# A state-space convolution and SwiGLU kernel on one core: a planned order that knows DMA lanes and dependent VectorE steps, merged opening loads, and the last product written over the kernel spectrum

## The chip, the cores and the metric

One Trainium2 chip, one core. The metric is the device time of one execution in microseconds (us), lower is better; several executions of each kernel are timed, and one further look is taken with the hardware profiler. Names used below: PE is TensorE (matmul), DVE is VectorE, ACT is ScalarE, POOL is GpSimd, SP is the engine that issues most DMA. The profile's *span* runs from the first to the last instruction and is some 1.8 us shorter than the device time of the same run.

An execution is called *fast* when it is within 1.5% of the fastest run of the same kernel, else *slow*; only fast runs are compared.

## The reference, cut to what matters

```python
# one batch, S = 2048 rows, D = 640, F = 1728, bf16
kv  = shift_conv4(k, shift_k) * v                 # 4-tap causal shift along S, then times v
y   = causal_conv(kv, ssm_k) + kv * ssm_D         # long convolution along S (written with rfft/irfft)
h   = q + layernorm(q) * y
out = h + (silu(layernorm(h) @ w_gate) * (layernorm(h) @ w_up)) @ w_down
```

## The kernel before

The sequence is cut into four blocks of 512 rows. The long convolution is done by block: each block of kv gets a trigonometric transform X(n) by matmul, each block of the kernel gets one G(p), combined into H(p), and the spectrum of output block n is A(n) = the sum of X(j)*H(n-j). Such a complex product of two 128x2560 halves is six or eight VectorE operations (`pair`). An inverse transform, two layer norms and an FFN follow for every block.

All instructions are first recorded in a plan with an engine, an estimated duration, dependencies and a priority. A greedy planner then simulates them and emits one fixed order for each engine; on the chip every engine works through its own list in that order. So the planner's model decides what stands behind what.

```python
    def order(self):                                   # the planner, cut
        free, dma, out = {}, 0.0, []
        while len(out) < n:
            # ... of all ready operations take the one that can start first, then by priority
            end = s + o["dur"]
            if o["kb"]:                                # a DMA: one common queue
                dma = max(dma, end + 1.3) + o["kb"] / RATE      # RATE = 270
                done = dma + 0.7
            for u in users[i]:                         # same engine: no delay
                lag = 0.0 if ops[u]["eng"] == e and not o["kb"] else 0.12
```

```python
    H = [slot[0], slot[4], slot[2], slot[3]]           # spectra of the kernel
    X = [slot[5], slot[6], slot[5], slot[6]]           # spectra of kv: X(2) reuses X(0)'s slot
    A = [slot[6], slot[7], slot[1], slot[7]]           # sums of products: A(3) reuses A(1)'s
    # ... pair(), the eight-operation form; T is one 128x2560 scratch tile
            vop(TM, T, U, U2, "T", xk + "c", gk + "c", pr)      # T  = U*U2
            vop(TA, Ac, Ac, T, ak + "c", "T", ak + "c", pr)     # Ac = Ac + T, reads what was just written
            vop(TM, T, V, V2, "T", xk + "s", gk + "s", pr)
            vop(TS, Ac, Ac, T, ak + "c", "T", ak + "c", pr)
            # ... the same twice more for As
```

Because X(2) needs X(0)'s slot, the products X(0)*H(2) and X(0)*H(3) have to be out of the way before X(2); the loop places them, and the products of X(1), right after the inverse transforms of blocks 1 and 2. Nothing but X(3)*H(0) is then left for block 3.

The opening loads k and v in one load a row tile, WG (the basis of G) in two halves, and the flip (a matrix that mirrors rows), WX (the basis of X) and x (the rows of q) loads with early priorities, most of them on ACT's queue, which also has to copy w4 (the broadcast shift weights) out of PSUM before VectorE can start.

## Time and profile before

| | before |
|---|---|
| median of the first three runs (range) | 335.8 us (332.1 to 337.7) |
| span of the profiled run | 328.4 us |
| first product of spectra on VectorE starts | 48.2 us |
| last spectral operation ends | 262.1 us |
| from there to the end | 66.3 us |

Busy time by stretch of the kernel before: opening, product stretch, end. Columns are the stretch and its length, then for each engine the busy us and the instruction count, then TensorE's granted clock (1.00 is full speed), the busy share of the DMA engines and GB/s.

```profile
core 0: us, PE busy (x) PEld busy (x) DVE busy (x) ACT busy (x) POOL busy (x), PEclk, DMA share, GB/s
0.00:48.20 48.20, 25.08 (x129) 14.79 (x130) 18.09 (x24) 21.41 (x40) 11.21 (x27) 0.93 0.95 256
48.20:262.10 213.90, 186.65 (x1065) 104.35 (x1077) 200.54 (x246) 121.87 (x233) 60.77 (x88) 0.97 0.47 133
262.10:328.40 66.30, 60.58 (x348) 32.98 (x350) 20.17 (x40) 23.15 (x46) 5.59 (x16) 1.00 0.30 78
```

In the middle line VectorE is busy 200.5 of 213.9 us and TensorE 186.7: VectorE bounds the stretch. In the last line it is TensorE alone. The total is the sum of the three lengths, so anything that moves the end of the second line moves the end of the kernel.

ACT's timeline in the opening of the kernel before. Columns: start, length, engine (ACTq is its DMA issue), source line, operation, and in brackets the idle time of ACT's compute before it with what ended it.

```profile
16.22 0.39 ACTq L252 DMA_DIRECT2D x<-in_A_q_dram  x1
16.64 1.28 ACT L278 ACT_TABLE_LOAD   x1 [16.64 <-DMA v<-in_A_v_dram]
17.94 1.29 ACT L278 CAST w<-psA 128x640 bf16<-128x640 f32 x2
...
26.02 0.34 ACTq L252 DMA_DIRECT2D WI<-const_wi  x1
26.40 1.29 ACT L294 CAST s0c<-psF 128x640 bf16<-128x640 f32 x2 [5.68 <-DMA wd<-in_A_ssm_k_dram]
```

ACT stands behind its own loads: the w4 copies come after the issue of x at 16.2, and the next copies after the issue of WI, which does not get out until 26.0.

VectorE in the product stretch of the kernel before:

```profile
106.35 1.49 DVE L356 TENSOR_TENSOR s<-s,T 128x2560 bf16<-128x2560 bf16 x1
107.76 0.42 DVE L494 TENSOR_TENSOR tT<-sg,uc 128x512 bf16<-128x512 bf16 x1
108.10 1.48 DVE L356 TENSOR_TENSOR T<-s6s,s0s 128x2560 bf16<-128x2560 bf16 x1
109.61 1.49 DVE L356 TENSOR_TENSOR s<-s,T 128x2560 bf16<-128x2560 bf16 x1
```

A 128x2560 operation takes 1.40 us start to start when the next does not need its result (106.35 to 107.76 shows 1.41), and 1.52 us when the next one reads it (108.10 to 109.61 shows 1.51). I call the difference, 0.115 us, a bubble. The step can be counted in a timeline: it is where the next operation starts after the printed end of the one before, by less than 0.15 us. There are 81 of them in the product stretch.

VectorE at the last X transform, then TensorE at the start of the third FFN, both of the kernel before:

```profile
245.94 0.43 DVE L494 TENSOR_TENSOR tT<-sg,uc 128x512 bf16<-128x512 bf16 x1 [4.92 <-ACT uc L492]
248.70 1.49 DVE L356 TENSOR_TENSOR T<-s6c,s0c 128x2560 bf16<-128x2560 bf16 x1 [2.33 <-ACT s6c L352]
```

```profile
205.68 0.45 PE L335 MATMUL psA<-kv,flip 128*128 128x320 bf16 x2
215.84 0.58 PE L485 MATMUL psF<-hT,wg 128*128 128x512 bf16 x1 [9.71 <-DVE s L356]
```

VectorE idles 4.92 and 2.33 us because no product is left to do; earlier, TensorE idles 9.71 us because the third FFN's input, hT, waits in VectorE's list.

### The profile page before, as it was taken

The numbers are of one execution on the slowest core, as the hardware profiler recorded it, in microseconds if no ns is written. First come the engines' busy times: TensorE is split into PE (matmuls) and PEld (weight loads), VectorE is DVE, ScalarE is ACT, GpSimd is POOL, SyncE is SP. The second block draws the span as 40 slices with busy tenths as digits, with TensorE's granted clock in tenths as the row PEclk, the third lists the DMA queues.
The fourth block names the chain that finished last, engine by engine and source line by source line (L and its number), as shares of the span: only waits on it lengthen the run. The fifth ranks groups of instructions, "written<-read, shape, count | busy, mean of one in ns | idle before, by whom it ended". The sixth has DMA issues, their size and how long they took to land.

```text
span 328.4 us, 4290 instructions
## 1 busy us (share of the span) xinstructions
PE 272.3 (83%) x1540; PEld 152.1 (46%) x1556; DVE 238.8 (73%) x307; ACT 166.4 (51%) x318; POOL 77.6 (24%) x131
## 2 busy tenths in 40 slices
PE   1066789995899988999989799169997998999995
PEld 0034546773345444654445366024453564444563
DVE  0049359998999999999999999999836984121122
ACT  0043998876256548116768217268465472355400
POOL 5000333650000004800580004579300033000000
PEclk9997979999799999999999999769999999999999
DMA  7999930239673507229992701516732405365011
GB/s 220 353 196 310 351 73 1 103 60 299 222 212 98 142 4 177 63 79 289 276 283 56 221 21 40 147 35 160 232 84 53 113 23 130 90 161 141 0 42 40
DMA packets 72121, 45.94 MB, mean 140 GB/s; under 512 B 30821, under 2 KB 69542, under 8 KB 72100
## 3 DMA queue, kind: packets, MB, share of 16 engines
q1 hardware_dynamic: 70160, 41.22, 45.9%
q10 hardware_dynamic: 1812, 4.38, 4.3%
q8 instruction: 12, 0.20, 0.2%
q0 software_dynamic: 128, 0.07, 0.1%
q14 instruction: 9, 0.07, 0.1%
HBM read 37.80 MB, written 2.62 MB: 123 GB/s over the span
## 4 chain that ended last, share of the span: by engine, by line
DVE 44%; PE 24%; issue 5%; ACT 4%; POOL 3%; DMA 1%; POOLq 0%; ACTq 0%; DVEq 0%; SPq 0%
PE psF L485 18%; DVE T L356 8%; DVE s L356 8%; DVE k L321 4%; PE psF L503 4%; DVE tT L494 2%; DVE k L322 2%; DVE s1s L356 2%; DVE o L508 2%; DVE s1c L356 2%; ACT uc L492 1%; DVE kv L324 1%; PE psA L349 1%; DVE x L452 1%; DVE k L323 1%
## 5 line engine op out<-in xcount | busy, mean ns | idle before, releaser
L485 PE MATMUL psF<-hT,wg 128*128 128x512 bf16 x269 | 70.6, 386 | 20.9 <-DVE s L356 9.7
L491 ACT ACTIVATE sg<-psF 128x512 bf16<-128x512 f32 (+1 forms) x56 | 33.4, 597 | 80.8 <-PE psF L485 76.6
L503 PE MATMUL psF<-wd,tT 128*128 128x320 bf16 x448 | 66.4, 299 | 1.2 <-ACT uc L492 1.2
L485 PE MATMUL psF<-hT,wu 128*128 128x512 bf16 x255 | 65.8, 386 | 0.8 <-ACT sg L491 0.4
L404 POOL TENSOR_TENSOR sm<-sm 128x1 f32<-128x1 f32 x28 | 13.9, 497 | 169.4 <-ACT junk L397 169.4
L503 PEld LDWEIGHTS <-tT 128*128 128x128 bf16 x448 | 41.5, 97 | 25.4 <-issue 8.7
L485 PEld LDWEIGHTS <-wg 128*128 128x128 bf16 x280 | 27.3, 99 | 53.8 <-issue 25.7
L494 DVE TENSOR_TENSOR tT<-sg,uc 128x512 bf16<-128x512 bf16 (+1 forms) x56 | 23.4, 419 | 34.7 <-ACT uc L492 34.5
L485 PEld LDWEIGHTS <-wu 128*128 128x128 bf16 x260 | 25.9, 100 | 31.6 <-issue 3.7
L492 ACT CAST uc<-psF 128x512 bf16<-128x512 f32 (+1 forms) x56 | 32.5, 580 | 3.7 <-PE psF L485 3.6
L291 PE MATMUL psF<-wd,s 128*128 128x320 bf16 x192 | 31.4, 325 | 3.3 <-ACT s0c L294 2.8
L291 PEld LDWEIGHTS <-s 128*128 128x128 bf16 x256 | 26.4, 104 | 16.2 <-issue 4.4
L321 DVE TENSOR_TENSOR k<-k,w 128x2560 bf16<-128x2560 bf16 x14 | 20.7, 1484 | 14.7 <-ACT w L278 14.7
L356 DVE TENSOR_TENSOR s<-s,T 128x2560 bf16<-128x2560 bf16 x20 | 29.8, 1488 | 0.4
L407 POOL TENSOR_TENSOR sm<-sm,mhalf 128x1 f32<-128x1 f32 x32 | 26.8, 837 | 2.7
L397 ACT ACTIVATE junk<-x 128x640 bf16<-128x640 bf16 x28 | 20.6, 737 | 10.5 <-DMA x<-in_A_q_dram 6.5
L349 PE MATMUL psA<-kv,WX 128*128 128x320 bf16 x128 | 21.5, 316 | 3.9 <-DVE kv L339 2.7
L508 DVE TENSOR_TENSOR o<-psF,x 128x640 bf16<-128x640 f32 x16 | 13.1, 819 | 12.3 <-PE psF L503 12.3
L398 ACT ACTIVATE junk<-x 128x640 bf16<-128x640 bf16 x28 | 20.7, 738 | 0.5
L349 PEld LDWEIGHTS <-WX 128*128 128x128 bf16 x128 | 13.1, 103 | 12.5 <-issue 3.0
L406 POOL TENSOR_SCALAR sm<-sm 128x1 f32<-128x1 f32 x28 | 17.8, 635 | 2.6 <-POOL sm L405 0.2
L405 POOL TENSOR_TENSOR sm<-sm 128x1 f32<-128x1 f32 x28 | 13.0, 464 | 18.2 <-ACT junk L398 17.1
(107 smaller groups left out, 309.4 us busy)
## 6 DMA issues: line engine op xcount, KB each, us to landing
k<-in_A_k_dram SPq DMA_DIRECT2D x12, 640.0 KB, 4.2
wg<-in_B_w_gate_dram SPq DMA_DIRECT2D x24, 320.0 KB, 3.2
wu<-in_B_w_up_dram SPq DMA_DIRECT2D x24, 320.0 KB, 3.8
out_dram<-o SPq DMA_DIRECT2D x16, 160.0 KB, 1.8
wd<-in_B_w_down_dram SPq DMA_DIRECT2D x1, 2080.0 KB
v<-in_A_v_dram SPq DMA_DIRECT2D x12, 160.0 KB, 4.2
x<-in_A_q_dram SPq DMA_DIRECT2D x3, 640.0 KB
s<-const_wg ACTq DMA_DIRECT2D x2, 512.0 KB, 8.7
```

Of the source, the lines that this page charges most:

```text
L291: nc.tensor.matmul(ps(g)[:, h, 0:NH], WG[:, kt, ct * P:(ct + 1) * P], gT[p][:, kt, h * NH:(h + 1) * NH], start=(kt == 0), stop=(kt == 3))
L321: add("DVE", dve(4 * D), lambda: nc.vector.tensor_mul(kd[:], kd[:], w4[:]), r=["w4"] + ks, w=[kn], pr=pr)
L349: nc.tensor.matmul(ps(g)[:, h, 0:NH], WX[:, kt, ct * P:(ct + 1) * P], kv[:, base + kt, h * NH:(h + 1) * NH], start=(kt == 0), stop=(kt == 1))
L356: add("DVE", dve(4 * D), lambda: f(o[:], a[:], b[:]), r=[ak, bk], w=[ok], after=["WG0", "WG1"] if ok[:2] == "s7" else [], pr=pr)
L397: add("ACT", act(D) + 0.2, lambda: nc.scalar.activation(junk[:], src, ACT.Copy, scale=1.0 / D, accum_out=s[:, 0:1]), r=[xk], w=[k + "a"], ...
L398: add("ACT", act(D) + 0.2, lambda: nc.scalar.activation(junk[:], src, ACT.Square, scale=float(D ** -0.5), accum_out=s[:, 1:2]), r=[xk], w= ...
L407: e.tensor_tensor(s[:, 4:5], s[:, 3:4], mhalf[:], op=ALU.pow)
L485: nc.tensor.matmul(ps(gr)[:, which, :], w[:, kt, cc * P:(cc + 1) * P], hT[b][:, kt, :], start=(kt == 0), stop=(kt == 4))
L491: add("ACT", act(MB), lambda gr=gr, s=s, z=z: nc.scalar.activation(sg[s][:z, :], ps(gr)[:z, 0, :], ACT.Silu), r=[(gr, 0)], w=[f"sg{s}"], p ...
L492: add("ACT", act(MB), lambda gr=gr, s=s, z=z, merged=merged: nc.scalar.copy(uc[s][:z, :], ps(gr)[64:128, 0, :] if merged else ps(gr)[:, 1, ...
L494: add("DVE", dve(MB), lambda c=c, s=s, z=z: TM(tT[:z, c * MB:(c + 1) * MB], sg[s][:z, :], uc[s][:z, :]), r=[f"sg{s}", f"uc{s}"], w=[f"tT{c ...
L503: nc.tensor.matmul(ps(gr)[:, h, 0:NH], tT[:z, c * MB + m * P:c * MB + (m + 1) * P], wd[:z, c, h * NH:(h + 1) * NH], start=(c == 0), stop=( ...
```

## The change

Its intent: make the planner (a) hold a load back until one of eight *lanes* is free (a lane is taken by each load not issued by POOL, until it has landed) and let the queues share one bandwidth; (b) start a dependent VectorE operation 0.12 us late, as the traces show it, so that independent ones are put between; (c) merge the loads of the opening so that fewer issues block ACT; (d) write the last product X(0)*H(3) over H(3), so that X(2), X(3) and A(3) get free slots and all products of a block but the last one can be done before its own X transform.

```diff
-        free, dma, out = {}, 0.0, []
+        free, dma, out, lanes = {}, {}, [], [0.0] * 8
+                    if o["kb"] and e != "POOL":
+                        s = max(s, lanes[0])
-                dma = max(dma, end + 1.3) + o["kb"] / RATE
-                done = dma + 0.7
+                begin = max(dma.get(e, 0.0), end + 1.3)
+                share = 1 + sum(f > begin for q, f in dma.items() if q != e)
+                dma[e] = begin + o["kb"] * share / RATE
+                done = dma[e] + 0.7
+                if e != "POOL":
+                    lanes = lanes[1:] + [done]
-                lag = 0.0 if ops[u]["eng"] == e and not o["kb"] else 0.12
+                lag = 0.0 if ops[u]["eng"] == e and e != "DVE" and not o["kb"] else 0.12
-RATE = 270.0
+RATE = 330.0
+MOVE = "add"
-    T = tl("T", [P, 4, D])
+    T = tl("T", [P, 8, D])          # two halves, Ta and Tb
-    X = [slot[5], slot[6], slot[5], slot[6]]
-    A = [slot[6], slot[7], slot[1], slot[7]]
+    X = [slot[5], slot[6], slot[7], slot[5]]
+    A = [slot[6], slot[7], slot[1], slot[3]]
# ... opening: SP's transposes are planned with 2.7 us of issue instead of 4.5; WG in one 1 MB load, v of block 0 in one load, k rows 256 to 511 in one 1.28 MB load,
# ... ssm_D moved to POOL's queue, an early Silu so that the table load comes first, t0 for flip, WX, WI
# ... pair(): products and sums alternate between Ta and Tb; "over" writes A over H(3);
# ... a variant that lets DMA do the additions is in the code, but MOVE = "add" leaves it unused
-                add("PE", ..., mm, r=["wdl", "wdl2"] + ...)
+                add("PE", ..., mm, r=["wdl", "wdl2", (("F", "U", n, 13), 0)] + ...)   # down after the last up
     for n in range(1, NB):
         front(n, z)
-        if n == 1:
-            pair(0, 1, z + 20, True)
         load_x(n, z - 100)
-        if n == 2:
-            pair(0, 3, z + 5, True)
+        pair(0, n, z + 20, "over" if n == 3 else "first")
+        for j in range(1, n):
+            pair(j, n - j, z + 22 + j, MOVE)
         x_transform(n, z + 30)
-        pair(n, 0, z + 40, False)
+        pair(n, 0, z + 40, "add")
         inverse(n, z + 50)
-# ... the products that stood here after the inverse are gone
```

More of the change, by code (lines that the diff above doesn't have):

```diff
@@ L109, in order @@
             if best is None:
-                for i, o in enumerate(ops):
-                    if "start" not in o: print(i, o["eng"], o["pr"], o["acq"], left[i], o["fn"].__qualname__, o["fn"].__code__.co_firstlineno)
                 raise RuntimeError("stuck")
@@ L191 @@
     J_h = nc.inline_tensor(make_flip(), name="const_flip")
-    slot = [[tl(f"s{i}{h}", [P, 4, D]) for h in "cs"] for i in range(7)]
-    last = tl("s7", [P, 8, D])
-    slot.append([last[:, 0:4, :], last[:, 4:8, :]])
-    T = tl("T", [P, 4, D])
+    slot = [tl(f"s{i}", [P, 8, D]) for i in range(8)]
+    last, fourth = slot[7], slot[4]
+    slot = [[t[:, 0:4, :], t[:, 4:8, :]] for t in slot]
+    T = tl("T", [P, 8, D])
+    Tk = [["T0", "T1"], ["T2", "T3"]]
     tT = tl("tT", [P, 14 * MB])
@@ L202 @@
     w4 = tl("w4", [P, 4, D])
-    wrow = T[0:1, :, :].rearrange("p a b -> p (a b)")
+    wrow = T[0:1, 0:4, :].rearrange("p a b -> p (a b)")
     ones = tl("ones", [1, P])
@@ L236 @@
     G = [slot[0], slot[1], slot[2], slot[3]]
-    X = [slot[5], slot[6], slot[5], slot[6]]
-    A = [slot[6], slot[7], slot[1], slot[7]]
+    X = [slot[5], slot[6], slot[7], slot[5]]
+    A = [slot[6], slot[7], slot[1], slot[3]]
     Hk, Gk = ["s0", "s4", "s2", "s3"], ["s0", "s1", "s2", "s3"]
-    Xk, Ak = ["s5", "s6", "s5", "s6"], ["s6", "s7", "s1", "s7"]
+    Xk, Ak = ["s5", "s6", "s7", "s5"], ["s6", "s7", "s1", "s3"]
     def r3(a):
@@ L257 @@
     load("ACT", wrow, A_shift_k.partition_broadcast(1).rearrange("o a b -> o (a b)"), ["wrow"], -100, 5)
-    load("ACT", drow, A_ssm_D.partition_broadcast(1), ["drow"], -99, 5)
+    add("ACT", 1.5, lambda: nc.scalar.activation(sg[0][0:1, 0:P], ones[:], ACT.Silu), r=["ones"], w=["sg0"], pr=-50)
+    load("POOL", drow, A_ssm_D.partition_broadcast(1), ["drow"], -75, 5)
     def gload(p, pr):
-        add("SP", 4.5, lambda: nc.sync.dma_start_transpose(gT[p], A_ssm_k[:, p * MB:(p + 1) * MB]), w=[f"gT{p}"], pr=pr, kb=640)
-    def wgload(i):
-        load("ACT", WG[:, 2 * i:2 * i + 2, :], WG_h.ap()[:, 2 * i:2 * i + 2, :], [f"WG{i}"], -39.5 + i, 512)
+        add("SP", 2.7, lambda: nc.sync.dma_start_transpose(gT[p], A_ssm_k[:, p * MB:(p + 1) * MB]), w=[f"gT{p}"], pr=pr, kb=640)
     gload(0, -90)
-    wgload(0)
-    wgload(1)
     def wcast(t):
@@ L299, in front_loads, with front_tile @@
         pass
-    def front_tile(n, q, pr, queue):
+    def front_tile(n, q, pr):
         b = q % 2
         r0 = n * MB + q * P
-        kd, kn = k4[b], f"k4_{b}"
-        if n == 0 and q > 1:
-            kd, kn = slot[4][b], "s4" + "cs"[b]
-        if n == 0 and q == 0:
-            add("POOL", 0.8, lambda: nc.gpsimd.memset(kd[0:32, :, :], 0.0), w=[kn], pr=-8)
-            for t in range(3):
-                k = 3 - t
-                load("POOL", kd[t:t + 1, k:4, :], kk[0:t + 1, :].rearrange("(o a) d -> o a d", o=1), [kn + f"x{t}"], -7, 2, r=[kn])
-            load("POOL", kd[3:16, :, :], bass.AP(tensor=kk.tensor, offset=kk.offset, ap=[[D, 13], [1, 4 * D]]).rearrange("p (a b) -> p a b", a=4), [kn + "x3"], -7, 65, r=[kn])
-            load(queue, kd[16:128, :, :], bass.AP(tensor=kk.tensor, offset=kk.offset + 13 * D, ap=[[D, 112], [1, 4 * D]]).rearrange("p (a b) -> p a b", a=4), [kn + "x4"], pr - 40, 560)
-        else:
-            load(queue, kd[:], bass.AP(tensor=kk.tensor, offset=kk.offset + (r0 - 3) * D, ap=[[D, P], [1, 4 * D]]).rearrange("p (a b) -> p a b", a=4), [kn] + [kn + f"x{i}" for i in range(5)], pr - 40, 640)
-        vb, vn = vt[b], f"v{b}"
-        if n == 0 and q > 1:
-            vb, vn = ot[b], f"o{b}"
-        load(queue, vb[:], vv[r0:r0 + P, :], [vn], pr - 40, 160)
-        ks = [kn] + [kn + f"x{i}" for i in range(5)]
+        kd, kn, vb, vn = k4[b], f"k4_{b}", vt[b], f"v{b}"
+        if n == 0:
+            vb, vn = hT[0][:].rearrange("p a b -> p (a b)")[:, q * D:(q + 1) * D], "v0all"
+            if q > 1:
+                kd, kn = slot[4][b], "s4" + "cs"[b]
+        else:
+            load("SP", kd[:], run(r0 - 3, P), [kn], pr - 40, 640)
+            load("SP", vb[:], vv[r0:r0 + P, :], [vn], pr - 40, 160)
+        ks = [kn] + [f"edge{i}" for i in range(5) if n == 0 and q == 0]
         add("DVE", dve(4 * D), lambda: nc.vector.tensor_mul(kd[:], kd[:], w4[:]), r=["w4"] + ks, w=[kn], pr=pr)
@@ L324, in front_tile, with run, first_loads, front @@
         add("DVE", dve(D), lambda: nc.vector.tensor_mul(kv[:, q, :], kd[:, 0, :], vb[:]), r=ks + [vn], w=[f"kv{q}"], pr=pr)
-    def front(n, pr, queue="SP"):
+    def run(row, n):
+        return bass.AP(tensor=kk.tensor, offset=kk.offset + row * D, ap=[[D, n], [1, 4 * D]]).rearrange("p (a b) -> p a b", a=4)
+    def first_loads():
+        kd = k4[0]
+        load("ACT", kd[16:128, :, :], run(13, 112), ["edge4"], -98, 560)
+        load("SP", k4[1][:], run(P - 3, P), ["k4_1"], -88, 640)
+        load("ACT", hT[0][:].rearrange("p a b -> p (a b)").rearrange("p (a b) -> p a b", a=4), vv[0:MB, :].rearrange("(m p) d -> p m d", p=P), ["v0all"], -97, 640)
+        load("ACT", WG, WG_h.ap(), ["WG0", "WG1"], -96, 1024)
+        load("SP", fourth[:].rearrange("p (m a) b -> p m (a b)", m=2),
+             bass.AP(tensor=kk.tensor, offset=kk.offset + (2 * P - 3) * D, ap=[[D, P], [P * D, 2], [1, 4 * D]]), ["s4c", "s4s"], -87, 1280)
+        add("POOL", 2.2, lambda: nc.gpsimd.memset(kd[0:32, :, :], 0.0), w=["k4_0"], pr=-90)
+        for t in range(3):
+            k = 3 - t
+            load("POOL", kd[t:t + 1, k:4, :], kk[0:t + 1, :].rearrange("(o a) d -> o a d", o=1), [f"edge{t}"], -80, 2, r=["k4_0"])
+        load("POOL", kd[3:16, :, :], run(0, 13), ["edge3"], -81, 65, r=["k4_0"])
+    def front(n, pr):
         for q in (0, 1, 2, 3):
-            front_tile(n, q, pr + q, queue if n or q < 2 else "SP")
+            front_tile(n, q, pr + q)
             if q < 2:
@@ L353, in x_transform, with vop @@
                 r=[g], w=[Xk[n] + "cs"[ct // 4]], pr=pr - 900, rel=("A", g))
-    def vop(f, o, a, b, ok, ak, bk, pr):
-        add("DVE", dve(4 * D), lambda: f(o[:], a[:], b[:]), r=[ak, bk], w=[ok], after=["WG0", "WG1"] if ok[:2] == "s7" else [], pr=pr)
+    def vop(f, o, a, b, ok, ak, bk, pr, n=4):
+        ks = lambda k: k if isinstance(k, list) else [k]
+        add("DVE", dve(n * D), lambda: f(o, a, b), r=ks(ak) + ks(bk), w=ks(ok), after=["WG0", "WG1"] if ok[:2] == "s7" else [], pr=pr)
     TA, TS, TM = nc.vector.tensor_add, nc.vector.tensor_sub, nc.vector.tensor_mul
@@ L361, in hbuild, with pair @@
         g, gp, d, gk, gpk, dk = G[p], G[p - 1], H[p], Gk[p], Gk[p - 1], Hk[p]
-        vop(TA, d[0], g[0], gp[1], dk + "c", gk + "c", gpk + "s", pr)
-        vop(TS, d[1], g[1], gp[0], dk + "s", gk + "s", gpk + "c", pr)
-    def pair(j, p, pr, first):
+        vop(TA, d[0][:], g[0][:], gp[1][:], dk + "c", gk + "c", gpk + "s", pr)
+        vop(TS, d[1][:], g[1][:], gp[0][:], dk + "s", gk + "s", gpk + "c", pr)
+    def pair(j, p, pr, how):
         x, g, a, xk, gk, ak = X[j], H[p], A[j + p], Xk[j], Hk[p], Ak[j + p]
-        (U, V), (U2, V2), (Ac, As) = x, g, a
-        if first:
-            vop(TM, Ac, U, U2, ak + "c", xk + "c", gk + "c", pr)
-            vop(TM, T, V, V2, "T", xk + "s", gk + "s", pr)
-            vop(TS, Ac, Ac, T, ak + "c", "T", ak + "c", pr)
-            vop(TM, As, U, V2, ak + "s", xk + "c", gk + "s", pr)
-        else:
-            vop(TM, T, U, U2, "T", xk + "c", gk + "c", pr)
-            vop(TA, Ac, Ac, T, ak + "c", "T", ak + "c", pr)
-            vop(TM, T, V, V2, "T", xk + "s", gk + "s", pr)
-            vop(TS, Ac, Ac, T, ak + "c", "T", ak + "c", pr)
-            vop(TM, T, U, V2, "T", xk + "c", gk + "s", pr)
-            vop(TA, As, As, T, ak + "s", "T", ak + "s", pr)
-        vop(TM, T, V, U2, "T", xk + "s", gk + "c", pr)
-        vop(TA, As, As, T, ak + "s", "T", ak + "s", pr)
@@ new lines, in pair @@
+        U, V, U2, V2, Ac, As = (t[:] for t in (*x, *g, *a))
+        Uk, Vk, U2k, V2k, Ack, Ask = (k + h for k in (xk, gk, ak) for h in "cs")
+        if how == "move":
+            for i in range(2):
+                c = slice(2 * i, 2 * i + 2)
+                for d, dk, f, (b0, b0k), (b1, b1k) in ((Ac, Ack, TS, (U2, U2k), (V2, V2k)), (As, Ask, TA, (V2, V2k), (U2, U2k))):
+                    e = 0 if d is Ac else 2
+                    t0, t1 = T[:, 2 * e:2 * e + 2, :], T[:, 2 * e + 2:2 * e + 4, :]
+                    k0, k1 = f"T{e}", f"T{e + 1}"
+                    vop(TM, t0, U[:, c, :], b0[:, c, :], k0, Uk, b0k, pr, 2)
+                    vop(TM, t1, V[:, c, :], b1[:, c, :], k1, Vk, b1k, pr, 2)
+                    vop(f, t0, t0, t1, k0, k0, k1, pr, 2)
+                    add("POOL", 1.1, lambda d=d, c=c, t0=t0: nc.gpsimd.dma_start(out=d[:, c, :].rearrange("p a b -> p (a b)"), in_=t0.rearrange("p a b -> p (a b)"),
+                                                                                accum_op=ALU.add, max_dma_last_dim=2560), r=[k0, dk], w=[dk], pr=pr, kb=640)
+            return
@@ new lines, in pair @@
+        Ta, Tb, Tak, Tbk = T[:, 0:4, :], T[:, 4:8, :], Tk[0], Tk[1]
+        if how == "over":
+            vop(TM, Ta, U, V2, Tak, Uk, V2k, pr)
+            vop(TM, Tb, V, V2, Tbk, Vk, V2k, pr)
+            vop(TM, As, V, U2, Ask, Vk, U2k, pr)
+            vop(TM, Ac, U, U2, Ack, Uk, U2k, pr)
+            vop(TA, As, As, Ta, Ask, Tak, Ask, pr)
+            vop(TS, Ac, Ac, Tb, Ack, Tbk, Ack, pr)
+            return
+        if how == "first":
+            vop(TM, Ac, U, U2, Ack, Uk, U2k, pr)
+            vop(TM, Ta, V, V2, Tak, Vk, V2k, pr)
+            vop(TM, As, U, V2, Ask, Uk, V2k, pr)
+            vop(TM, Tb, V, U2, Tbk, Vk, U2k, pr)
+            vop(TS, Ac, Ac, Ta, Ack, Tak, Ack, pr)
+            vop(TA, As, As, Tb, Ask, Tbk, Ask, pr)
+            return
@@ L383, in ln @@
+        vop(TM, Ta, U, U2, Tak, Uk, U2k, pr)
+        vop(TM, Tb, V, V2, Tbk, Vk, V2k, pr)
+        vop(TA, Ac, Ac, Ta, Ack, Tak, Ack, pr)
+        vop(TM, Ta, U, V2, Tak, Uk, V2k, pr)
+        vop(TS, Ac, Ac, Tb, Ack, Tbk, Ack, pr)
+        vop(TM, Tb, V, U2, Tbk, Vk, U2k, pr)
+        vop(TA, As, As, Ta, Ask, Tak, Ask, pr)
+        vop(TA, As, As, Tb, Ask, Tbk, Ask, pr)
     def ln(n, q, which, pr, vec=False):
@@ L414, in load_x @@
     def load_x(n, pr, queue="SP"):
-        load(queue, xin[n % 2][:], xq[n * MB:(n + 1) * MB, :].rearrange("(m p) d -> p m d", p=P), [f"x{n % 2}_{q}" for q in range(4)], pr, 640, t0=30 if n == 1 else 0)
+        load(queue, xin[n % 2][:], xq[n * MB:(n + 1) * MB, :].rearrange("(m p) d -> p m d", p=P), [f"x{n % 2}_{q}" for q in range(4)], pr, 640, t0=(10, 30, 0, 0)[n])
         for q in range(4):
@@ L456, in inverse @@
                 add("SP", 1.3, lambda q=q, half=half: nc.sync.dma_start_transpose(hT[b][:, :, q * P:(q + 1) * P], hl[half][:]),
-                    r=[hk], w=[f"hT{b}_{q}"], after=["gT3"] if n == 1 else [], pr=pr, kb=160)
+                    r=[hk], w=[f"hT{b}_{q}"], after=[["v0all"], ["gT3"], [], []][n], pr=pr, kb=160)
     wcount = [0]
@@ L504, in mm @@
                                              wd[:z, c, h * NH:(h + 1) * NH], start=(c == 0), stop=(c == 13))
-                add("PE", 2 * (c1 - c0) * 0.137, mm, r=["wdl", "wdl2"] + [f"tT{c}" for c in range(c0, c1)] + ([(gr, i - 1)] if i else []),
+                add("PE", 2 * (c1 - c0) * 0.137, mm, r=["wdl", "wdl2", (("F", "U", n, 13), 0)] + [f"tT{c}" for c in range(c0, c1)] + ([(gr, i - 1)] if i else []),
                     w=[(gr, i)], pr=pr + 20 + m, acq=("F", gr) if i == 0 else None)
@@ L510, in ffn @@
             load("SP", oo[r0:r0 + P, :], ot[s][:], [], pr - 300, 160, r=[f"o{s}"])
-    load("ACT", flip[:], J_h.ap(), ["flip"], -26, 64)
+    load("ACT", flip[:], J_h.ap(), ["flip"], -26, 64, t0=6)
+    first_loads()
+    load("ACT", WX[:], WX_h.ap(), ["WX"], -25, 512, t0=8)
     g_transform(0, -5)
-    front(0, 0, "ACT")
+    front(0, 0)
     gload(1, -30)
-    load("ACT", WX[:], WX_h.ap(), ["WX"], -25, 512)
     gload(2, -20)
@@ L520 @@
     gload(3, -10)
-    load("ACT", WI[:], WI_h.ap(), ["WI"], -5, 512)
+    load("ACT", WI[:], WI_h.ap(), ["WI"], -5, 512, t0=16)
     x_transform(0, 8)
-    pair(0, 0, 10, True)
+    pair(0, 0, 10, "first")
     inverse(0, 20)
@@ L535 @@
         front(n, z)
-        if n == 1:
-            pair(0, 1, z + 20, True)
         load_x(n, z - 100)
-        if n == 2:
-            pair(0, 3, z + 5, True)
+        pair(0, n, z + 20, "over" if n == 3 else "first")
+        for j in range(1, n):
+            pair(j, n - j, z + 22 + j, MOVE)
         x_transform(n, z + 30)
-        pair(n, 0, z + 40, False)
+        pair(n, 0, z + 40, "add")
         inverse(n, z + 50)
-        if n == 1:
-            pair(0, 2, z + 500, True)
-            pair(1, 1, z + 510, False)
-        if n == 2:
-            pair(1, 2, z + 500, False)
-            pair(2, 1, z + 510, False)
         ffn(n - 1, 1000 * n + 500)
```

## The prediction

> **What bounds the kernel.** The table of stretches splits the 328.4 us span. 0 to 20 us: DVE 0.5 and PE 2.6 us busy, DMA 98%: opening. 48.2 (first product of spectra) to 262.1 (end of the last): DVE busy 200.5 of 213.9 us, PE 186.7. After that PE: inverse, layer norm and transposes to 278.4, then the last FFN. So DVE bounds the middle, and the end follows its last spectral operation by 66.3 us.
>
> Three losses ahead of that point:
> 1. Opening. ACT issues loads in order and stands behind them until 16.6 us (waits table: 16.6 us, put down to a v load); only then come the four copies that make w4, so DVE starts at 20.76. ACT blocks again until 26.0. X transform starts at 40.0, first spectral product at 48.2.
> 2. Bubbles. In the DVE timeline 128x2560 operations start 1.40 us apart when independent, 1.52 when one reads its predecessor's result. I count 94 such steps before 262, 0.115 us each: 11 us. The Trainium skill (VectorE: DVE Perf Modes, "The DRAIN you can't avoid") says a semaphore between operations costs nothing extra; this trace differs.
> 3. DVE idle 8.3 us at 235 to 249 (1.05 + 4.92 + 2.33), waiting for FFN copies and the last X transform with no other product left. PE also stands 9.7 us at 206 and 4.5 at 78 for transposed hT.
>
> **What the change does.** The DVE count stays 307; arithmetic and bytes stay. The DMA-accumulate variant is switched off. Merged loads: ACT has four loads, then the table load, so w4 is ready near 11 us. New costs: "ones" is set after five POOL DMA issues (about 6 us), and DVE's first operation waits for a small POOL load, near 12 us. The next two transposes no longer wait and share the DMA engines with k, v and WG. The skill (DMA: Bandwidth & Descriptors, "Issuing engines are not separate DMA queues") says all queues share the same 16 engines; 4.9 MB at about 300 GB/s (opening slices) lands WG at 16 to 18 us, so G products start only 2 us earlier but run unblocked. I estimate X transform at 31, first product near 39.5: 8 to 9 us.
> Bubbles: adjacent reads of the preceding result fall from 96 to 39 in program order: 6 to 7 us, all in the DVE-bound stretch.
> The last product goes over the spectrum's own slot, X(2) and X(3) get free slots, so other products fill DVE during the last X transform: 4 to 6 of the 8.3. A block's down-projections are held together behind its last up-projection (112 matmuls, 15 us), covering the layer-norm chain; the 9.7 us PE wait should go, worth little as DVE bounds. At the end 40 down matmuls instead of 76 cover the last layer norm: PE waits about 5 us more there, not additive.
>
> Sum: last spectral operation at 262 - 8.5 - 6.5 - 5 = 242, plus 66 = 308, less a little front work done earlier: span about 306. PE needs about 250 us from 18 us on, so it has room. Before is 335.8 median; I predict 310 us, range 302 to 320; faster 0.96, same 0.03, slower 0.01.
>
> **What would show it.** DVE's first 128x2560 at 12 to 14 us; first spectral product near 39; 30 to 40 steps at 1.52; last spectral operation near 242; no PE wait over 5 us at about 200; a PE wait of 5 to 7 us before the last FFN; last spectral operation to end still 65 to 67.
>
> **What would make it wrong.** WG or the merged k load landing after 20 us; in-order queues that mismatch the planned times, so DVE stalls at FFN products waiting for ACT; a lower granted clock; slow runs.

## The result

| | before | after |
|---|---|---|
| median (range, runs) | 333.9 us (328.7 to 337.7, 4) | 311.6 us (311.2 to 312.6, 4) |
| span of the profiled run | 328.4 | 310.8 |
| first product starts | 48.2 | 44.6 |
| length of the product stretch | 213.9 | 198.1 |
| dependent steps in it | 81 | 8 |
| VectorE idle over 0.15 us in it | 10.0 | 6.4 |
| last spectral operation to the end | 66.3 | 68.1 |

The ratio of the fast runs is 0.944 (95% interval 0.935 to 0.953). A ratio is the mean time of one kernel's fast runs over that of the other's of the same rounds, so it is not quite the ratio of the medians in the table; two of the four runs of the kernel before in it, 335.8 and 337.7, count as slow and are left out.

The same three stretches of the changed kernel:

```profile
core 0: us, PE busy (x) PEld busy (x) DVE busy (x) ACT busy (x) POOL busy (x), PEclk, DMA share, GB/s
0.00:44.60 44.60, 23.96 (x138) 14.76 (x139) 20.70 (x30) 23.15 (x42) 14.18 (x28) 0.96 0.95 277
44.60:242.70 198.10, 188.90 (x1101) 105.69 (x1099) 191.32 (x242) 118.21 (x231) 92.83 (x88) 0.99 0.53 145
242.70:310.80 68.10, 58.63 (x320) 30.99 (x319) 19.11 (x38) 23.15 (x46) 5.49 (x17) 0.94 0.28 73
```

The product stretch is 15.8 us shorter, the opening 3.6, and the end 1.8 longer. In the middle line TensorE is now busy 188.9 and VectorE 191.3 of 198.1 us: both are nearly full at the same time.

ACT and TensorE in the opening of the changed kernel:

```profile
10.86 1.29 ACT L280 CAST w<-psA 128x640 bf16<-128x640 f32 x2 [2.61 <-DMA k<-in_A_k_dram]
...
29.82 0.33 ACTq L258 DMA_DIRECT2D WI<-const_wi  x1
```

```profile
18.97 10.53 PE L293 MATMUL psF<-wd,s 128*128 128x320 bf16 x64 [9.95 <-DMA s<-const_wg]
...
29.61 2.34 PE L293 MATMUL psF<-wd,s 128*128 128x320 bf16 x16
31.79 0.43 PE L347 MATMUL psA<-kv,flip 128*128 128x320 bf16 x2
36.09 3.98 PE L361 MATMUL psA<-kv,WX 128*128 128x320 bf16 x16 [3.87 <-DMA WI<-const_wi]
```

The w4 copies no longer stand behind x and WI. But the first G product still waits for WG until 18.97 (19.93 before), and the X transform starts at 36.09. The profile names the WI load as what ended that wait, yet these matmuls read WX and kv; VectorE's own timeline shows what they read:

```profile
32.98 0.83 DVE L350 TENSOR_TENSOR kv<-kv,rev 128x1280 bf16<-128x1280 bf16 x1 [7.96 <-ACT rev L349]
33.73 1.49 DVE L315 TENSOR_TENSOR k<-k,w 128x2560 bf16<-128x2560 bf16 x1
35.13 0.82 DVE L351 TENSOR_TENSOR kv<-kv,rev 128x1280 bf16<-128x1280 bf16 x1
```

The second kv operation (source line 351) starts at 35.13 and takes 0.82, so it ends at 35.95, just ahead of 36.09. It is late twice: the second flip product on TensorE stands behind 16 G matmuls (29.61 to 31.79), and the planner, knowing now that a dependent operation starts late, put a 1.49 us operation of the next block into the 0.12 us gap between the two kv operations. (That operation also reads a load of the next block, so that a late load can hold up the first X transform too.)

VectorE in the product stretch of the changed kernel:

```profile
208.54 1.48 DVE L369 TENSOR_TENSOR T<-s,s 128x2560 bf16<-128x2560 bf16 x1
209.94 1.48 DVE L369 TENSOR_TENSOR s<-s,T 128x2560 bf16<-128x2560 bf16 x1
211.34 0.41 DVE L533 TENSOR_TENSOR tT<-sg,uc 128x512 bf16<-128x512 bf16 x1
211.68 1.48 DVE L369 TENSOR_TENSOR T<-s,s 128x2560 bf16<-128x2560 bf16 x1
```

A product into one half of T and a sum from the other follow each other at 1.40 us: the bubble is gone.

TensorE at the start of the last FFN of the changed kernel, then the stretches around it with the granted clock:

```profile
247.07 5.91 PE L542 MATMUL psF<-wd,tT 128*128 128x320 bf16 x40
258.74 2.29 PE L524 MATMUL psF<-hT,wg 128*128 128x512 bf16 x5 [5.77 <-DMA hT<-hl]
...
264.93 1.24 PE L524 MATMUL psF<-hT,wu 128*128 128x512 bf16 x5
```

```profile
core 0: us, PE busy (x) PEld busy (x) DVE busy (x) ACT busy (x) POOL busy (x), PEclk, DMA share, GB/s
...
253.00:258.70 5.70, 0.00 (x0) 0.00 (x0) 1.72 (x3) 1.14 (x4) 1.82 (x6) 0.93 0.61 131
258.70:265.00 6.30, 6.26 (x16) 2.32 (x17) 0.42 (x1) 1.07 (x2) 0.00 (x0) 0.52 0.00 0
265.00:271.00 6.00, 6.00 (x30) 2.70 (x29) 0.85 (x2) 2.62 (x5) 0.00 (x0) 1.00 0.45 119
```

After a wait of 5.77 us for hT, the first three groups of five matmuls take 6.19 us (258.74 to 264.93) where the next three take 3.24 (264.93 to 268.17), and the granted clock of that stretch is 0.52.

### The profile page after: what moved, and what is told of

It reads as the page before. It is cut to its first block, busy times and chain, and to the rows that moved or that the text cites. A ratio compares the mean times of both kernels' runs of the same rounds, so it can differ in the third digit from the quotient of the medians.

```text
span 310.8 us, 4298 instructions
## 1 busy us (share of the span) xinstructions
PE 271.5 (87%) x1556; PEld 151.4 (49%) x1556; DVE 231.1 (74%) x307; ACT 164.5 (53%) x318; POOL 112.5 (36%) x132
## 4 chain that ended last, share of the span: by engine, by line
PE 40%; DVE 32%; DMA 9%; ACT 7%; POOL 6%; issue 5%; ACTq 0%; POOLq 0%; DVEq 0%
PE psF L524 23%; DVE s L369 10%; PE psF L542 8%; DMA s<-const_wg 5%; DVE T L369 4%; PE psF L293 4%; PE psA L361 3%; DVE k L315 3%; DMA hT<-hl 3%; DMA WI<-const_wi 2%; DVE tT L533 2%; DVE y L490 2%; POOL sm L443 2%; ACT junk L436 2%; POOL sm L445 2%
## 5 line engine op out<-in xcount | busy, mean ns | idle before, releaser
L443 POOL TENSOR_TENSOR sm<-sm 128x1 f32<-128x1 f32 x28 | 39.5, 1411 | 117.9 <-ACT junk L436 117.9
L524 PE MATMUL psF<-hT,wg 128*128 128x512 bf16 x280 | 72.3, 390 | 9.4 <-DMA hT<-hl 7.5
L542 PE MATMUL psF<-wd,tT 128*128 128x320 bf16 x448 | 64.9, 299 | 1.1 <-ACT uc L531 0.9
L369 DVE TENSOR_TENSOR T<-s,s 128x2560 bf16<-128x2560 bf16 x32 | 47.2, 1482 | 0.0
L369 DVE TENSOR_TENSOR s<-s,T 128x2560 bf16<-128x2560 bf16 x32 | 47.2, 1482 | 0.0
L293 PE MATMUL psF<-wd,s 128*128 128x320 bf16 x192 | 29.3, 310 | 10.3 <-DMA s<-const_wg 10.0
L293 PEld LDWEIGHTS <-s 128*128 128x128 bf16 x256 | 25.6, 100 | 21.9 <-DMA s<-const_wg 10.6
L446 POOL TENSOR_TENSOR sm<-sm,mhalf 128x1 f32<-128x1 f32 x32 | 32.8, 1024 | 2.7
L296 ACT CAST s<-psF 128x640 bf16<-128x640 f32 x32 | 22.1, 695 | 17.1 <-PE psF L293 17.0
L547 DVE TENSOR_TENSOR o<-psF,x 128x640 bf16<-128x640 f32 x16 | 13.1, 817 | 12.5 <-PE psF L542 12.5
L364 ACT CAST s<-psA 128x640 bf16<-128x640 f32 x32 | 21.3, 704 | 0.9 <-PE psA L361 0.8
```

The source lines that it names most:

```text
L293: nc.tensor.matmul(ps(g)[:, h, 0:NH], WG[:, kt, ct * P:(ct + 1) * P], gT[p][:, kt, h * NH:(h + 1) * NH], start=(kt == 0), stop=(kt == 3))
L369: add("DVE", dve(n * D), lambda: f(o, a, b), r=ks(ak) + ks(bk), w=ks(ok), after=["WG0", "WG1"] if ok[:2] == "s7" else [], pr=pr)
L443: e.tensor_tensor(s[:, 2:3], s[:, 0:1], s[:, 0:1], op=ALU.mult)
L446: e.tensor_tensor(s[:, 4:5], s[:, 3:4], mhalf[:], op=ALU.pow)
L524: nc.tensor.matmul(ps(gr)[:, which, :], w[:, kt, cc * P:(cc + 1) * P], hT[b][:, kt, :], start=(kt == 0), stop=(kt == 4))
L542: nc.tensor.matmul(ps(gr)[:, h, 0:NH], tT[:z, c * MB + m * P:c * MB + (m + 1) * P], wd[:z, c, h * NH:(h + 1) * NH], start=(c == 0), stop=( ...
```

## The experiments

Each is an edit of the changed kernel unless said otherwise. Times are medians of four runs (one with the profiler, three timed), all of them fast but for one of e2_opening (314.4; its three fast ones have a median of 310.3) and two of the kernel before. The changed kernel itself had 311.6 us. The columns after the median are of one execution each, the profiled one, whose own time is given: it is the slowest of its four for the changed kernel and the fastest for e1b_both and e2_opening. Dependent steps are counted from the trace's records; a printed timeline, which merges equal lines, hides a few of them (67 of 69 for e1b_both, the number that the recorded texts use).

| run | edit | median us | profiled run us | first product | stretch | dependent steps | VectorE idle | last to end |
|---|---|---|---|---|---|---|---|---|
| before | | 333.9 | 330.2 | 48.2 | 213.9 | 81 | 10.0 | 66.3 |
| after | | 311.6 | 312.6 | 44.6 | 198.1 | 8 | 6.4 | 68.1 |
| e1a_lag | no lag in the planner | 312.4 | 313.2 | 43.9 | 199.1 | 54 | 3.1 | 68.3 |
| e1b_both | and one half of T | 312.8 | 311.1 | 42.5 | 198.7 | 69 | 0.4 | 68.1 |
| e2_opening | old loads | 311.6 | 309.0 | 41.6 | 197.2 | 8 | 2.6 | 68.4 |
| e3_slots | old slots | 318.4 | 319.1 | 45.2 | 204.9 | 9 | 13.0 | 67.2 |
| g1_slots_bubbles | e1b and e3 | 322.8 | 322.3 | 43.6 | 207.8 | 75 | 7.5 | 69.1 |
| h2_light_bubbles | e1b, fewer gate and up matmuls | 304.0 | 303.4 | 43.6 | 200.0 | 71 | 1.5 | 58.1 |
| e5_gate | down not held back | 312.8 | 312.3 | 45.4 | 197.3 | 9 | 5.1 | 67.8 |
| e4_warm | filler matmuls | 308.9 | 309.1 | 45.7 | 196.4 | 8 | 4.8 | 65.2 |
| e7_open | tighter opening | 313.6 | 314.1 | 41.4 | 200.5 | 11 | 8.5 | 70.5 |

The profiles of e26_opening_lanes, h1_light and f1_lanes fell in slow runs, so they have no line. Runs of one job shared a chip; the jobs had three different chips, and the kernel before had medians of 333.0, 334.1 and 340.0 in them. The changed kernel was not run again in these jobs, so differences of 1 us from its 311.6 show nothing.

### e1a_lag and e1b_both: the bubbles back

```diff
-                lag = 0.0 if ops[u]["eng"] == e and e != "DVE" and not o["kb"] else 0.12
+                lag = 0.0 if ops[u]["eng"] == e and not o["kb"] else 0.12
# e1b_both also, in pair():
-        vop(TM, Ta, U, U2, ...); vop(TM, Tb, V, V2, ...); vop(TA, Ac, Ac, Ta, ...); ...
+        vop(TM, Ta, U, U2, ...); vop(TA, Ac, Ac, Ta, ...); vop(TM, Ta, V, V2, ...); ...
```

> The changed kernel, but ordered with no lag between dependent VectorE operations (products still use two halves of T). In program order 73 operations wait for and read their immediate predecessor instead of 24. Theory (bubbles cost 0.115 us each on the bounding engine): about 50 more steps at 1.52 us, last spectral operation about 5.5 us later than 242.7, time about 317 us (311.6 before this edit). Rival (the gain in the middle came from the free slots; bubbles are absorbed by waits elsewhere): under 313 us.

> As the run before it, and the products also go through one half of T in the old order (product, add, product, add). 82 such waits. Theory: dependent steps in the product stretch back from 8 to about 75 to 80, last spectral operation about 8 us later, time 319 to 320 us. Rival: under 314 us.

The steps came back (54 and 69), the time did not: 312.4 and 312.8 us. My theory falls as stated. The product stretch of e1b_both:

```profile
42.50:241.20 198.70, 187.52 (x1101) 106.23 (x1100) 195.54 (x241) 119.45 (x233) 73.80 (x90) 0.99 0.52 145
```

It is 198.7 us long against 198.1. VectorE is busy 195.5 us instead of 191.3, and its idle went from 6.4 to 0.4: the bubbles took the place of idle time. New theory: with the new slots, TensorE's work sets almost the same length as VectorE's, so taking bubbles out leaves VectorE waiting.

A second candidate lies in the same traces, and I did not test it. Of VectorE's 6.4 us of idle in the changed kernel, 3.7 ended with ACT's FFN copies, which follow TensorE's matmuls, but 2.7 ended with the layer-norm scalars that POOL makes; in e1b_both the whole idle, 0.4, is POOL's. One POOL operation of the changed kernel, and all engines while it ran (columns as above):

```profile
204.62 18.01 POOL L443 TENSOR_TENSOR sm<-sm 128x1 f32<-128x1 f32 x1 [12.51 <-ACT junk L436]
```

```profile
204.70:222.50 17.80, 17.11 (x92) 8.78 (x90) 17.80 (x19) 14.18 (x29) 17.80 (x1) 1.00 0.44 113
```

A 128x1 operation of this kind takes 0.19 us at the shortest, and at most 2.0 in the kernel before and 1.5 in e1b_both. Here it took 18.0, VectorE had no gap meanwhile, and it ended 0.05 us after VectorE's first gap (222.58). POOL's 88 operations of the stretch took 92.8 us where those of the kernel before took 60.8 (a profile is rough on POOL). This suggests that bubbles let POOL through and that removing them slows the layer norms; it is not shown by an experiment.

### e2_opening: the old loads back

```diff
-    load("ACT", WG, WG_h.ap(), ["WG0", "WG1"], -96, 1024)     # and the other merged loads
+    wgload(0); wgload(1)                                      # two halves, one load for each k and v tile
+    # ssm_D on ACT's queue, no early Silu, no t0
```

> The changed kernel with the loads of the opening as they were (k, v and WG in separate loads, no early table load, ssm_D on ACT's queue); slots, order rules and halves of T stay. Theory: first spectral product 3.6 us later as in the two profiles (48.2 against 44.6), all of it on the chain, time 315 to 316 us. Rival (the new order also needs the early w4 to fill VectorE, so the opening is worth more): 318 us or more. Rival 2 (opening absorbed later): under 313 us.

311.6 us, and in its profile the first product even came earlier, at 41.6. Rival 2: the merged loads as such are worth nothing that shows in the end, though with runs from 309.0 to 314.4 us a gain of 1 or 2 us would not show. With the lanes in the planner, ACT's list has the w4 copies (14.20 to 16.99 in the trace) ahead of flip, WX and x in this kernel; in the changed kernel they are ahead of x alone. The profiled run is the fastest, 309.0 us: in it the 3 us of the opening were kept to the end, as its last spectral operation came at 238.8 instead of 242.7.

### e3_slots: the old slots back

```diff
-    X = [slot[5], slot[6], slot[7], slot[5]]
-    A = [slot[6], slot[7], slot[1], slot[3]]
+    X = [slot[5], slot[6], slot[5], slot[6]]
+    A = [slot[6], slot[7], slot[1], slot[7]]
# and the products at their old places in the loop
```

> The changed kernel with the old slots for X(2), X(3), A(3) and the products at their old places in the plan; nothing is written over the spectrum. Theory: VectorE again has no product left during the last X transform, idle 6 to 8 us there against none, last spectral operation 4 to 7 us later, time 316 to 318 us. Rival (the scheduler fills the hole with other work, slots are worth nothing): within 1 us of 311.6.

318.4 us, 6.8 more, as the theory had it (its upper end was 318). Product stretch, then TensorE, then VectorE of this kernel:

```profile
45.20:250.10 204.90, 182.71 (x1057) 102.13 (x1056) 191.44 (x241) 119.91 (x231) 68.16 (x88) 0.96 0.49 139
```

```profile
208.61 2.29 PE L524 MATMUL psF<-hT,wg 128*128 128x512 bf16 x5 [14.06 <-DMA hT<-hl]
```

```profile
234.28 0.42 DVE L533 TENSOR_TENSOR tT<-sg,uc 128x512 bf16<-128x512 bf16 x1 [3.97 <-ACT uc L531]
237.04 2.89 DVE L369 TENSOR_TENSOR T<-s,s 128x2560 bf16<-128x2560 bf16 x2 [2.33 <-ACT s L364]
```

VectorE idles 3.97 and 2.33 us at the last X transform again, and before that TensorE waits 14.06 us for hT, after which its first 15 matmuls take 5.94 us (208.61 to 214.55) instead of 3.24: the slow restart that the changed kernel has before its last FFN. TensorE's busy time in the stretch is 182.7 of 204.9: the two take turns again. So the slots do more than fill one hole: they let the products of a block stand where TensorE has work of its own.

### g1_slots_bubbles: both back

The edits of e1b_both and e3_slots together.

> The changed kernel with both the bubbles (as e1b_both) and the old slots (as e3_slots). e1b alone cost 1 us with 67 dependent steps in the stretch, e3 alone 6.8 us (318.4). New theory (with both parts in, TensorE is as full as VectorE, so 7 us of bubbles only fill idle VectorE time; with the old slots VectorE alone bounds again): bubbles now show, time 323 to 326 us. Rival (bubbles are not a cost at all on this chain): 318 to 320 us.

322.8 us, just under my interval, and 4.4 above e3_slots. With the old slots the bubbles cost; with the new ones they cost about 1 us or nothing. (e3_slots ran on another chip; the 4.4 us are clear of the 2 to 3 us range of either kernel's runs, and the fast runs of the kernel before have means of 329.0 and 328.7 us on the two chips.)

### h1_light and h2_light_bubbles: less work for TensorE

Their outputs are wrong, which doesn't matter for the times.

```diff
-                    for kt in range(5):
+                    for kt in range(3):
                         nc.tensor.matmul(ps(gr)[:, which, :], w[:, kt, ...], hT[b][:, kt, :],
-                                         start=(kt == 0), stop=(kt == 4))
+                                         start=(kt == 0), stop=(kt == 2))
# h1: in the changed kernel; h2: in e1b_both
```

> Wrong result on purpose: the changed kernel with 3 of the 5 matmuls of every up-projection (planner not told, so the same order). TensorE loses 216 matmuls, about 47 us of work, 35 of them before the last spectral operation. Theory (TensorE now bounds the middle together with VectorE): VectorE's idle in the product stretch falls from 6.4 to under 3 us, the stretch from 198 to about 193 us. Rival (TensorE does not bound): stretch within 1.5 us of 198.

> Wrong result on purpose: e1b_both with the same light up-projections. Theory (bubbles cost what the steps show once TensorE is out of the way): product stretch near 198 to 199, 5 to 7 us longer than h1_light, and the time 4 to 7 us above h1_light. Rival (bubbles cost nothing): within 2 us of h1_light.

h1_light had two fast runs, 297.6 and 299.4 us, and two slow ones, the profiled one among them, so what I expected of its stretch can't be read (in the slow profile it was 194.4 us with 3.5 us of VectorE idle, which settles nothing). h2_light_bubbles had 303.4 to 304.7, all fast. By the fast runs the bubbles cost 5 to 6 us with TensorE lightened, against about 1 us or nothing with its full work. The product stretch of h2_light_bubbles:

```profile
43.60:243.60 200.00, 164.04 (x939) 92.56 (x938) 195.76 (x241) 118.29 (x233) 70.30 (x90) 0.95 0.52 143
```

It is as long as that of e1b_both (200.0 against 198.7) with 23 us less TensorE work in it: with bubbles, VectorE bounds alone. Lightening gained 8.8 us with bubbles (312.8 to 304.0), no more than the shorter end gives (58.1 instead of 68.1 us), and 13.1 without them (311.6 to the mean of h1's two fast runs). This supports the theory that it is TensorE's load that hides most of the bubbles, though only two fast runs stand for h1, h1 and h2 also differ in order, and POOL's waits are not separated by it.

### e26_opening_lanes and f1_lanes: the planner's model of DMA

e26 is e2_opening with the old DMA model in the planner. f1 is the kernel *before* with the new model alone:

```diff
+                    if o["kb"] and e != "POOL":
+                        s = max(s, lanes[0])       # and the per-queue dma[e], RATE = 330, as in the change
```

> The changed kernel with the old loads of the opening and the old model of DMA in the planner (one queue at 270, no lanes). With the old loads alone nothing was lost (311.6) and the first product came at 41.6. Theory (the order worked out with lanes is what mends the opening, the merged loads are not needed for it): first product back near 47 to 48, time 314 to 316 us. Rival (neither matters for the end): within 1.5 us of 311.6.

> The kernel before with one part of the change alone: the planner's model of DMA lanes and shared queues. Loads, slots, bubbles and down-projections as before. The plan now puts the four w4 copies ahead of the flip, WX and x loads on ACT's queue. Theory (the opening is mended by this order, not by merged loads): first spectral product at 41 to 43 us instead of 48.2, fast runs 5 to 7 us below the kernel before of the same job, about 321 to 323 us. Rival (the merged loads are what mends the opening): first product after 46 us, time within 2 us of before.

e26: one fast run, 317.7 us, and three slow ones, 323.1 to 327.6. The fast one is 6 us above e2_opening's median, so the model of lanes is worth about that much where the old loads are used; one run is little to rest on, and its first product can't be compared, as the profile fell in a slow run. (The order in a list is the plan's, slow or fast: in e26's trace the w4 copies stand behind x again, in f1's they are ahead of flip, WX and x, so both edits did what they should.) f1: a median of 337.7 us where the kernel before had 340.0 in the same job, slow runs included; the ratio of the fast runs is 1.004 (0.987 to 1.022): no gain shown. The theory that lanes alone mend the kernel before falls. What the lanes are worth by themselves stays open.

### e5_gate: down-projections free again

```diff
-                r=["wdl", "wdl2", (("F", "U", n, 13), 0)] + ...
+                r=["wdl", "wdl2"] + ...
```

> The changed kernel with down-projections free to start before the block's last up-projection, as in the kernel before. Only the last two blocks' order changes (some 20 matmuls of down-projection move ahead of the last up-projections). Theory (this rule is worth nothing by itself): 311 to 312.5 us. Rival (it matters for the end, as the last block's chain is TensorE alone): over 313 us.

312.8 us, between the two expectations, 1.2 us above the changed kernel's median of another job. Not settled; small in any case.

### e7_open: a tighter opening

```diff
-                add("PE", 2 * 0.137, mm, r=["flip", f"kv{q}"], w=[g], pr=pr, ...)
+                add("PE", 2 * 0.137, mm, r=["flip", f"kv{q}"], w=[g], pr=pr if n else -60, ...)
# and no lag for the second kv operation; x_transform(0, -6) instead of 8
```

> The changed kernel with a tighter opening: the flip products of block 0 go ahead of the rest of the kernel spectrum on TensorE, and the second kv operation follows the first without a slot for another between them. Theory (X transform waits for kv, not for data): X transform starts at 29 to 31 instead of 36.1, first product at 38 to 39 instead of 44.6; as TensorE also bounds afterwards, time 3 to 6 us lower, 306 to 309 us. Rival (absorbed, TensorE bounds alone): under 1 us.

The X transform started at 32.67 and the first product moved from 44.6 to 41.4, both less than I expected; the time did not move: 313.6 us. The stretch became 200.5, with 8.5 us of VectorE idle, so the last spectral operation ended at 241.8 instead of 242.7. The end was 2.4 us longer besides: 56 down matmuls (8.08 us) were left between the last inverse and the wait for hT, where the changed kernel had 40 (5.91). Of the idle, 8.1 us ended with POOL's scalars, the longest part after a POOL operation that ran from 144.26 to 163.48 while VectorE had no gap:

```profile
144.26 19.22 POOL L443 TENSOR_TENSOR sm<-sm 128x1 f32<-128x1 f32 x1 [18.30 <-ACT junk L436]
```

```profile
167.38 0.80 DVE L451 TENSOR_SCALAR xln<-x,sm 128x640 bf16<-128x640 bf16 x2 [3.95 <-POOL sm L446]
```

Three us of opening were given back by later waits, most of them for POOL. As the planner then made other choices in the whole list, this does not show that every earlier opening would be lost.

### e4_warm: TensorE kept busy

```diff
+    def keep_warm():
+        for i in range(24):
+            nc.tensor.matmul(ps(("F", "K"))[:, 0, :], WI[:, 0, 0:P], ...512 columns of WI..., start=True, stop=True)
+    add("PE", 24 * 0.217, keep_warm, r=[(("F", "D", NB - 2, 3), 3)], ...)   # between the last two FFNs
     ffn(NB - 1, 1000 * NB + 500)
```

> The changed kernel with 24 matmuls of no use (results never read) put on TensorE behind the last block's predecessor's down-projection, to fill the 5.8 us wait for hT at 253 to 259 us. Theory (TensorE's slow first 15 matmuls after that wait, 6.2 us instead of 3.2, come from the wait itself): the last FFN runs at 1.08 us a group from its start, time 2.5 to 3 us lower, about 308.7 us. Rival (they are slow for another reason): time as before it or, if they delay the FFN, up to 1 us higher.

308.9 us (307.9 to 309.1), correct, and 2.7 below the changed kernel: the best version here. The changed kernel had run in another job; e5_gate, which is within about 1 us of it, had 312.8 us in the same job as e4_warm. TensorE of this kernel:

```profile
252.34 5.36 PE L586 MATMUL psF<-WI 128*128 128x512 bf16 x23
258.19 1.24 PE L524 MATMUL psF<-hT,wg 128*128 128x512 bf16 x5 [0.49 <-DMA hT<-hl]
259.26 1.24 PE L524 MATMUL psF<-hT,wu 128*128 128x512 bf16 x5
```

The filler ends just before hT lands, and the last FFN starts at 1.08 us a group. The granted clock from 258.1 to 264.0 is 1.00, and the end of the kernel is 65.2 us instead of 68.1.

## Why the prediction was right or wrong

The total was right: 310 us predicted, 311.6 measured, and the last spectral operation at 242.7 where I had 242. That is luck in part: its terms were not all right, and their errors cancel.

- *Opening, 8 to 9 us.* Too large; the profiles show 3.6. The step that failed is "G products start only 2 us earlier but run unblocked. I estimate X transform at 31". G did run unblocked, but started at 18.97 instead of 16 to 18, and X started at 36.1 because the kv operations were late. I had read the order of the lists and not followed the flip products through TensorE's. What 3 us of it are worth stays open: e2_opening and e7_open both had first products 3 us earlier than the changed kernel; the profiled run of e2_opening was faster by 3.7 us, its median was not, and e7_open lost them to later waits.
- *Bubbles, 6 to 7 us, "all in the DVE-bound stretch".* The count was better than I predicted (8 dependent steps left, not 30 to 40), and 73 steps at 0.115 are 8.4 us of VectorE time. But the words "DVE-bound" failed: after the change VectorE waits for the other engines instead (for TensorE, which h1 and h2 support; for POOL, which the traces suggest), and the bubbles are worth about 1 us or nothing there. With the old slots they are worth 4.4 us.
- *Slots, 4 to 6 us.* Measured 6.8 by e3_slots. I counted only the idle hole at the last X transform. The 9.71 us wait of TensorE at 206, which I called "worth little as DVE bounds", belongs to the same ill: in e3_slots it returned as 14.06 us. That it would go was right: between 80 and 250 us TensorE waits at most 1.74 us in the changed kernel.
- *End, 66 us.* The wait of 5.8 us before the last FFN came as predicted (5 to 7). "Not additive" was wrong by 2.9 us: after that wait TensorE ran at half speed, and e4_warm took the cost away by filling the wait.
- *The product stretch.* Bubbles and slots were predicted to take 11 to 12 us out of it. It lost 15.8. In VectorE's time this is 8.4 of bubbles, 3.6 of idle and the rest, 3.8, mostly work moved ahead of the first product; the last I had put at "a little". That surplus made up for the opening.

Undone one on top of the other, the parts go 311.6, 318.4 (slots), 322.8 (and bubbles); e26's fast run adds about 6 for the opening and the planner's lanes. Their sum, an estimate and not a run, is about 329, inside the kernel before's fast runs of 327.1 to 331.5 on those two chips. So the parts do not simply add: bubbles or loads can be undone alone for about 1 us or nothing, and the slots cannot.

What I cited of the Trainium skill: "DMA: Bandwidth & Descriptors", section "Issuing engines are not separate DMA queues", fits the opening, where the queues of SP, ACT and POOL together took 0.95 of the DMA engines' time until the first product; no run here tests it. For "VectorE: DVE Perf Modes", section "The DRAIN you can't avoid", see the last section. The slow restart agrees with "TensorE: Matmul & The Clock Gate", section "Part 1: The HAM clock gate (the 'warmup' mystery)", which has the clock fall to half after an idle window of about 3.4 us: here a wait of 5.77 us was followed by 0.52 and one of 0.49 us, in e4_warm, by none. How short a wait can do it is another matter: see the last section. I did not look at that page before predicting, and it would have told me that the wait is additive.

Open: whether gapless VectorE work holds POOL up, and what that costs (a run with a gap left every few operations would tell); what the lanes are worth alone; why the time varies so much less after the change; what makes a run slow (all three slow profiles have their first product at 50.9 to 51.1 us and DMA at 97 to 151 GB/s from 20 to 30 us, where before, after and e2_opening have 276 to 309); whether e4_warm's filler and another opening together gain more.

## What to carry to other kernels

When two engines have nearly the same work, a saving on one of them shows only if the other one's work can be moved under it; here free buffers, which let products stand where TensorE is busy, were worth more than 73 removed bubbles. Test each part of a change by taking it out of the finished kernel and also in pairs: parts that seem worth nothing alone can be worth 4 us where the others are missing. When an engine loses its gaps, look at what the others did in them: here single POOL operations grew to 18 and 19 us. Look for waits of several us in front of a TensorE-bound tail, as they can cost once for the wait and once more for the clock.

## What the Trainium skill lacked or had wrong

- "VectorE: DVE Perf Modes", section "The DRAIN you can't avoid", tells of copies that take the same time with a semaphore after each or after the last only. It lacks the cost of a dependent step: here 128x2560 operations start 1.40 us apart, and 1.52 when one reads the result of the one before it. (It does not say whether its copies depend on one another, so "this trace differs" in the prediction says too much.)
- "TensorE: Matmul & The Clock Gate", section "Why this matters for your kernels", says to avoid idle gaps of over about 3 us. A shorter one is not always safe: in the changed kernel a wait of 1.74 us (to 134.77) was followed by a clock of 0.51 from 135.0 to 138.4, though in e4_warm one of 1.60 us was not. It lacks that a short run of matmuls without use is a remedy in the middle of a kernel: 24 of 512 columns took 5.4 us of otherwise idle time, and the kernel took 308.9 us instead of 311.6.
- No page has it that a greedy plan with a dependency lag may put a long operation into a short gap: here one of 1.49 us went into a gap of 0.12 us between two operations on the chain.
